# The order of ten score products in a fused attention and feed-forward kernel, and the maxima taken from them

## The chip, the core and the metric

The kernel runs on one core of a Trainium2 chip. A core has a matrix engine (TensorE, PE in the profile, with its weight loads as a row of their own, PEld), a vector engine (VectorE, DVE), an activation engine (ScalarE, ACT), a general engine (GpSimd, POOL), and a queue that issues DMAs (SyncE, SP). Each engine runs its own instructions in the order of the program and waits for others by semaphores. TensorE writes its results to PSUM, eight banks of 512 floats on each of 128 partitions; VectorE and ScalarE read them there. The metric is the device time of one execution in microseconds (us), the median of several runs.

## What is computed

Block-causal attention over 8 batches with 8 heads each, 576 positions of 64 numbers, and behind it a feed-forward layer of width 2048 with a SiLU between its two products:

```python
scores = 0.125 * q @ k^T                     # 576 x 576 for each head
mask: block_i >= block_j, blocks of 64
attn = exp(scores - max) / (sum + 1e-09)
x = (attn @ v), heads side by side           # 4608 x 512
h = x @ w_in;  out = (h / (1 + exp(-h))) @ w_out
```

## The kernel before

A float32 product is made of reduced-precision ones: a number is split into a high part and the rest, and high by high, high by rest and rest by high are added up in PSUM. The attention of the first two blocks of 64 queries is done early and apart. The other 448 queries of each head are the work of a **unit**, u0 to u63, one for each head of each batch. In the stretch from about 80 to 553 us the units run one behind another, mixed with the first feed-forward product of the batches that are done (token `ffn`, line 1071). Behind it comes the second feed-forward product (line 1148).

The order of all of this on every engine is written out by hand: ORDER is a list of tokens such as `u48.scores`, which are run in turn, and each engine gets its instructions in that order. No scheduler moves anything. Around the hand-over from unit 47 to unit 48 it reads:

```python
u47.gather u46.sums:1 keep u47.top ffn u45.inverse u47.spread u48.split_q save u47.wide ffn keep u50.load u47.sub:0 u47.sub:1
u47.exp:0 u48.scores save u47.sub:2 u47.exp:1 u48.max:0 u47.exp:2 u47.pv u48.max:1 u49.split_hi u47.add:0 u48.max:2 u47.add:1
```

What a unit does, step by step:

- `split_hi`, `split_k`, `split_q` (lines 690 to 703): ScalarE and GpSimd make the high parts and the rests of q and k.
- `scores` (line 705): ten products on TensorE, the score of keys by queries, turned so that 128 keys lie on the partitions. There are five groups of keys. Each sees only the queries that its mask allows, so its products are 448, 448, 320, 192 or 64 wide; each group has two products (with q's high part, and with its rest), each with a weight load ahead of it. SEG says for each piece which group of keys it is, its first column, its first query and its width; PASSES says the order of the ten products.
- Three PSUM banks take them (BANKS): the first holds the piece of 448 queries of key group 0, the second the pieces of 320 and 192, the third the other piece of 448 and the one of 64. Four banks go round: with `(3 * u.i + k) % NS`, a unit's second bank is the first bank of the unit before, and its third bank is the second bank of the unit before.
- `max:0`, `max:1`, `max:2` (line 719, the instruction is in the helper at line 656): VectorE takes maxima over the keys of each 32 from the banks into Mx; `half_max` (line 748) does the half-masked squares of 64 keys, two at a time; the last reduction makes mj (line 731).
- `gather`, `top`, `spread`, `wide`: the maxima of the four groups of 32 partitions are brought together by copies on ScalarE (mj, m), reduced, spread again and broadcast to MR.
- `sub:0`, `sub:1`, `sub:2` (line 758): VectorE subtracts the maxima from the scores of the first, second and third bank; this is the last reading of a bank. `sub:1` and `sub:2` end with a `half_sub` (line 752, instruction at 754). The order of sub:1 and sub:2 differs from unit to unit.
- `exp`, `add`, `sums`: ScalarE takes the exponentials (line 771), GpSimd and VectorE their sums. `pv` (line 816) multiplies them with v, `mult` divides by the sums, `x_hi` and `x_lo` make the rows of x.

Semaphores guard a bank as a whole: a reader waits for the last product that is written to the bank, the next writer for its last reader.

```python
SEG = [(0, 0, 0, 448), (2, 448, 128, 320), (3, 768, 256, 192), (1, 960, 0, 448), (4, 1408, 384, 64)]
PASSES = [(i, k, (0, 128)) for i in range(5) for k in range(2)]
BANKS = [(0, 448), (448, 960), (960, 1472)]
```

Of the kernel before, what the change touches and what calls it, by code (L numbers as in the profile page):

```python
# [14 lines left out]
ALU = mybir.AluOpType  # L15
# [41 lines left out]
SEG = [(0, 0, 0, 448), (2, 448, 128, 320), (3, 768, 256, 192), (1, 960, 0, 448), (4, 1408, 384, 64)]  # L57
COLS = 1472

if ROWS:  # L60
    LOWS = [(64, 0, 256), (0, 256, 576)]
    FULL, LOW, HIGH = (0, 128), (0, 64), (64, 128)
    PASSES = [(0, 0, FULL), (1, 0, FULL), (2, 0, FULL), (0, 1, LOW), (1, 1, HIGH), (2, 1, HIGH), (3, 0, FULL), (3, 1, FULL), (4, 0, FULL), (4, 1, FULL)]
else:
    LOWS = [(64, 0, 576)]
    PASSES = [(i, k, (0, 128)) for i in range(5) for k in range(2)]
PV = [0, 3, 1, 2, 4]
BANKS = [(0, 448), (448, 960), (960, 1472)]

# [368 lines left out]
def blocks32(ap):  # L438
    return ap.rearrange("p (b r) -> p b r", r=32)
# [9 lines left out]
def attn_ffn(ctx: ExitStack, tc: tile.TileContext, qk, v, qk0, v0, qk1, v1, w_in, w_out, out):  # L449
# [46 lines left out]
    Mx = sp.tile([P, NQB, 5], F32, tag="Mx", name="Mx")  # L496
# [157 lines left out]
    def ttr(out, in_, op):  # L654

        nc.vector.tensor_reduce(out=out, in_=in_, axis=AX.X, op=op, apply_transpose=True)  # L656
# [12 lines left out]
    class Unit:  # L669
# [35 lines left out]
        def scores(u):  # L705
            banks = [bank((0, 1, 2, 3, "C")[(3 * u.i + k) % NS]) for k in range(3)]

            def ps(c, w, r=P):
                i = max(i for i in range(3) if BANKS[i][0] <= c)
                return banks[i][:r, c - BANKS[i][0] : c - BANKS[i][0] + w]  # L710

            u.ps = ps
            for seg, qq, r in PASSES:
                j, c, q0, w = SEG[seg]
                m = min(P, S - j * P)
                q, r = (u.qh, u.ql)[qq], slice(*r)
                nc.tensor.matmul(u.ps(c, w, m), u.kk[r, j * P : j * P + m], q[r, q0 : q0 + w], start=qq == 0 and not (ROWS and seg == 2), stop=qq == 1 and not (ROWS and seg == 1), skip_group_check=ROWS)  # L717

        def max(u, k):
            if k == 0:  # L720
                ttr(Mx[:, :, 0], blocks32(u.ps(0, NQ)), ALU.max)
            elif k == 1:
                for j, c, q0, w in SEG[1:3]:
                    ttr(Mx[:, q0 // 32 + 2 :, j], blocks32(u.ps(c + 64, w - 64)), ALU.max)
                u.half_max(0)
            else:
                j, c, q0, w = SEG[3]
                ttr(Mx[:, q0 // 32 + 2 :, j], blocks32(u.ps(c + 64, w - 64)), ALU.max)
                u.half_max(1)
                u.mj = sp.tile([P, 4, NQB], F32, tag="mj", name="mj")  # L730
                nc.vector.tensor_reduce(out=u.mj[:, 0], in_=Mx, axis=AX.X, op=ALU.max)
# [510 lines left out]
    for token in ORDER.split():  # L1242
# [3 lines left out]
        elif method:  # L1246
            method, _, k = method.partition(":")
# [47 lines left out]
```

## Time and profile before

| | |
|---|---|
| median of 3 runs | 989.66 us (989.62 to 989.88) |
| span of the profiled execution | 987.9 us |
| TensorE: products, weight loads | 978.8 us, 887.4 us busy |
| VectorE, ScalarE, GpSimd | 790.0, 688.6, 596.7 us busy |
| the 640 score products (line 717) | first at 80.6, last at 545.4 us |
| maxima (line 656, Mx) | 384 instructions, 130.0 us |

The profile shows one execution, from its first instruction to its last; the 1.8 us between its span and the median of the runs lie around it. A row of a timeline has the start, the time taken, the engine, the line, the operation, what is written and read, its shape and count; idle time of the engine ahead of it stands in brackets with what ended it. Rows of equal instructions that follow each other are merged. Products overlap and their ends are modelled, so the start of one and the start of the next say more than the time taken.

### The profile page before, as it was taken

How to read it: one execution, taken by the hardware profiler on the slowest of the kernel's cores; microseconds unless marked ns; L12 is line 12 of the kernel's file. 1: busy time of each engine (PE TensorE's matmuls, PEld its weight loads, DVE VectorE, ACT ScalarE, POOL GpSimd, SP SyncE). 2: the span in 40 equal slices, each digit the busy share in tenths (PEclk: the TensorE clock that was granted, in tenths of full speed). 3: DMA queues.
4: the chain of work that ended last, by engine and by line, in shares of the span. 5: the costliest groups of instructions: out<-in, count | busy, mean ns of one | idle time of the engine just before them, and what ended most of it. 6: DMA issues, size and time to landing. Idle time of an engine off the chain costs nothing.

```text
span 987.9 us, 20770 instructions
## 1 busy us (share of the span) xinstructions
PE 978.8 (99%) x6938; PEld 887.4 (90%) x6938; DVE 790.0 (80%) x2001; ACT 688.6 (70%) x1525; POOL 596.7 (60%) x706
## 2 busy tenths in 40 slices
PE   8999999999999999999999999999999999999998
PEld 7788778888888888888988899999999999999998
DVE  6977998999989899989999766788667767776651
ACT  4867767777777777777777556987666666666650
POOL 5558886877878878877787444554433434344430
PEclk9999999999999999999999999999999999999999
DMA  9965455556555556555554467555445444454411
GB/s 356 373 188 177 142 160 143 157 141 169 152 146 162 148 152 160 145 157 155 143 165 126 141 205 219 193 158 157 130 114 150 129 129 129 126 151 123 127 54 44
DMA packets 109803, 155.51 MB, mean 157 GB/s; under 512 B 18560, under 2 KB 83072, under 8 KB 109696
## 3 DMA queue, kind: packets, MB, share of 16 engines
q1 hardware_dynamic: 109696, 154.18, 52.7%
q8 instruction: 55, 0.90, 0.4%
q14 instruction: 52, 0.43, 0.1%
HBM read 106.95 MB, written 47.19 MB: 156 GB/s over the span
## 4 chain that ended last, share of the span: by engine, by line
PE 95%; DMA 3%; DVE 1%; SPq 0%; issue 0%; ACT 0%; DVEq 0%
PE h L1071 40%; PE S L1148 26%; PE c L1148 10%; PE S L717 9%; PE U L822 5%; PE SC L822 4%; DMA qk<-in_qk_dram 1%; DMA wst<-in_moe_w_in_dram 1%; DMA v<-in_v_dram 1%; PE S L1002 0%; PE S L1043 0%; PE S L879 0%; DVE SC L560 0%; DVE SC L556 0%; DVE wm L566 0%; DVE rr L1023 0%
## 5 line engine op out<-in xcount | busy, mean ns | idle before, releaser
L1071 PE MATMUL h<-x,wi 128*128 128x448 f32 (+2 forms) x1968 | 418.9, 369 | 0.0
L1071 PEld LDWEIGHTS h<-x,wi 128*128 128x128 f32 x1968 | 357.9, 188 | 34.6 <-issue 0.5
L656 DVE TRANSPOSE_TENSOR_REDUCE Mx<-S 64x4 f32<-64x128 f32 (+4 forms) x384 | 130.0, 396 | 7.6 <-PE S L717 6.9
L771 ACT ACTIVATE p<-T 128x512 f32<-128x512 f32 (+1 forms) x192 | 114.7, 613 | 26.7 <-DVE T L760 16.7
L1077 ACT COPY g<-h 128x448 f32<-128x448 f32 (+1 forms) x160 | 86.4, 540 | 38.7 <-PE h L1071 27.5
L777 POOL TENSOR_TENSOR pa<-p 128x448 f32<-128x448 f32 x64 | 73.7, 1151 | 61.1 <-ACT p L771 59.0
L1136 POOL TENSOR_TENSOR x<-raw,x 128x512 fp32r<-128x512 f32 (+1 forms) x58 | 58.8, 1017 | 80.6 <-ACT x L1132 74.9
L1136 POOL TENSOR_TENSOR wi<-raw,wi 128x512 fp32r<-128x512 f32 (+1 forms) x56 | 56.8, 1019 | 75.9 <-ACT wi L1132 71.3
L698 POOL TENSOR_TENSOR qh<-qk,qh 64x576 fp32r<-64x576 f32 x64 | 91.2, 1424 | 9.0 <-POOL pa L780 3.7
L717 PE MATMUL S<-qh 128*128 128x448 f32 (+3 forms) x320 | 92.6, 302 | 0.0
L717 PE MATMUL S<-ql,qh 128*128 128x448 f32 (+3 forms) x320 | 83.7, 306 | 0.0
L692 ACT CAST qh<-qk 128x1024 fp32r<-128x1024 f32 x64 | 67.1, 1049 | 23.1 <-PE S L717 9.5
L1099 ACT ACTIVATE raw<-raw 128x1024 f32<-128x1024 f32 x72 | 76.5, 1063 | 0.0
L702 POOL TENSOR_TENSOR ql<-qk,qh 128x448 fp32r<-128x448 f32 x64 | 73.7, 1151 | 3.8 <-ACT qh L692 1.0
L763 DVE TENSOR_TENSOR T<-S,MR 128x256 f32<-128x256 f32 (+2 forms) x192 | 73.5, 410 | 0.0
L717 PEld LDWEIGHTS S<-ql,qh 128*128 128x128 f32 (+1 forms) x320 | 57.0, 178 | 6.3 <-POOL ql L702 0.2
L717 PEld LDWEIGHTS S<-qh 128*128 128x128 f32 (+1 forms) x320 | 56.9, 178 | 3.3
L780 POOL TENSOR_TENSOR pa<-pa,p 128x320 f32<-128x320 f32 x64 | 55.9, 874 | 4.9 <-ACT p L771 0.2
L1148 PE MATMUL S<-tb,x 128*128 128x256 f32 x450 | 58.8, 283 | 0.0
L1136 POOL TENSOR_TENSOR gc<-raw,gc 128x512 fp32r<-128x512 f32 (+1 forms) x30 | 30.4, 1018 | 43.4 <-ACT gc L1132 39.6
L1148 PEld LDWEIGHTS S<-tb,x 128*128 128x128 f32 x450 | 56.1, 192 | 0.0
L742 ACT COPY m<-m 32x14 f32<-32x14 f32 x192 | 38.8, 202 | 22.0 <-DVE m L738 20.0
(211 smaller groups left out, 2063.6 us busy)
## 6 DMA issues: line engine op xcount, KB each, us to landing
qk<-in_qk_dram SPq DMA_DIRECT2D x128, 256.0 KB, 3.8
gdb<-g SPq DMA_DIRECT2D x128, 224.0 KB, 2.3
raw<-gdb SPq DMA_DIRECT2D x64, 256.0 KB, 3.2
v<-in_v_dram SPq DMA_DIRECT2D x64, 160.0 KB, 2.5
wst<-in_moe_w_in_dram SPq DMA_DIRECT2D x16, 512.0 KB, 8.6
wst<-in_moe_w_out_dram SPq DMA_DIRECT2D x16, 512.0 KB, 4.4
gd<-g SPq DMA_DIRECT2D x32, 256.0 KB, 3.6
raw<-gd SPq DMA_DIRECT2D x32, 256.0 KB, 3.5
```

The source lines that it names most:

```text
L656: nc.vector.tensor_reduce(out=out, in_=in_, axis=AX.X, op=op, apply_transpose=True)
L698: nc.gpsimd.tensor_tensor(out=u.qh[r, c], in0=u.raw[r, c], in1=u.qh[r, c], op=ALU.subtract)
L702: nc.gpsimd.tensor_tensor(out=u.ql, in0=u.raw[:, :NQ], in1=u.qh[:, :NQ], op=ALU.subtract)
L717: nc.tensor.matmul(u.ps(c, w, m), u.kk[r, j * P : j * P + m], q[r, q0 : q0 + w], start=qq == 0 and not (ROWS and seg == 2), stop=qq == 1 a ...
L771: nc.scalar.activation(u.p[:, c:e], u.T[:, c:e], AF.Exp, scale=SCALE)
L777: nc.gpsimd.tensor_tensor(out=u.pa, in0=u.p[:, :NQ], in1=u.p[:, 960 : 960 + NQ], op=ALU.add)
L822: nc.tensor.matmul(U[64 * e : 64 * e + 64, q0 : q0 + w], y.vv[:, e, j], z.p[:, c : c + w], start=n == 0, stop=n == 4)
L1071: nc.tensor.matmul(o, wi[wt][:, c, w], x_of(g, c, xt), start=c + k == 0, stop=c == CT - 1 and k == 2)
L1077: nc.scalar.copy(g, hs.pop(z)[:, :n])
L1099: nc.scalar.activation(u.raw, u.raw, AF.Silu)
L1136: e.tensor_tensor(out=u.goal(1, k), in0=u.source(k), in1=u.goal(0, k), op=ALU.subtract)
L1148: nc.tensor.matmul(o, quarter(u.g[a], j)[:, P * e : P * e + P], quarter(turned[d].g[b], TORDER[FACTOR[pr]]), start=u.q == 0 and i % 2 == 0 ...
```

## The change

The five pieces are computed in the order 0, 3, 1, 2, 4 of SEG, by falling width: 448, 448, 320, 192, 64, two products each. The third bank's wide piece moves ahead of both pieces of the second bank; the 64-wide piece, in the third bank too, stays last. The maxima are regrouped: max:1 now takes the wide piece of the third bank, and max:2 takes the two pieces of the second bank and both half-masked sets. ORDER is the same, and so are the numbers computed.

```diff
 else:
     LOWS = [(64, 0, 576)]
-    PASSES = [(i, k, (0, 128)) for i in range(5) for k in range(2)]
+    PASSES = [(i, k, (0, 128)) for i in (0, 3, 1, 2, 4) for k in range(2)]
...
             if k == 0:
                 ttr(Mx[:, :, 0], blocks32(u.ps(0, NQ)), ALU.max)
             elif k == 1:
+                j, c, q0, w = SEG[3]
+                ttr(Mx[:, q0 // 32 + 2 :, j], blocks32(u.ps(c + 64, w - 64)), ALU.max)
+            else:
                 for j, c, q0, w in SEG[1:3]:
                     ttr(Mx[:, q0 // 32 + 2 :, j], blocks32(u.ps(c + 64, w - 64)), ALU.max)
                 u.half_max(0)
-            else:
-                j, c, q0, w = SEG[3]
-                ttr(Mx[:, q0 // 32 + 2 :, j], blocks32(u.ps(c + 64, w - 64)), ALU.max)
                 u.half_max(1)
```

TensorE at unit 48, before and after with the semaphores waited for. S_6117, S_6118 and S_6119 are the unit's first, second and third bank; the sign - marks rows of before, + rows of the change:

```order
 L717 MATMUL S_6117<-qh 128x448 [waits Pool_49]
 L717 MATMUL S_6117<-ql,qh 128x448 [waits Pool_49]
-L717 MATMUL S_6118<-qh 128x320 [waits DVE_49]
+L717 MATMUL S_6119<-qh 128x448 [waits DVE_49,PE_49]
+L717 MATMUL S_6119<-ql,qh 128x448
+L717 MATMUL S_6118<-qh 128x320
 L717 MATMUL S_6118<-ql,qh 128x320
 L717 MATMUL S_6118<-qh 128x192
 L717 MATMUL S_6118<-ql,qh 128x192
-L717 MATMUL S_6119<-qh 128x448 [waits DVE_49,PE_49]
-L717 MATMUL S_6119<-ql,qh 128x448
 L717 MATMUL S_6119<-qh 64x64
```

The two 448-wide products of the third bank, and the wait for VectorE that they carry, moved from the seventh and eighth place to the third and fourth. The wait that the second bank's first product had of its own is gone, since the third bank's covers it.

VectorE at the same unit, its maxima:

```order
 L656 TENSOR_REDUCE Mx<-S_6117 128x14 [waits PE_49]
-L656 TENSOR_REDUCE Mx<-S_6118 128x8 [waits PE_49]
+L656 TENSOR_REDUCE Mx<-S_6119 128x12 [waits PE_49]
+L656 TENSOR_REDUCE Mx<-S_6118 128x8
 L656 TENSOR_REDUCE Mx<-S_6118 128x4
 L656 TENSOR_REDUCE Mx<-S_6118 64x2x2
-L656 TENSOR_REDUCE Mx<-S_6119 128x12 [waits PE_49]
 L656 TENSOR_REDUCE Mx<-S_6119 64x2x2
 L731 TENSOR_REDUCE mj<-Mx 128x14 [waits DVE_49]
```

The reduction of the third bank moved ahead of the three of the second; it is now the second one of the unit and the last that waits for TensorE. ScalarE, GpSimd and the DMA queue have the same instructions in the same order as before.

## The prediction

> **What bounds the kernel now.** I began with the page's table of busy times and then asked for the same times in three stretches: start, attention (0.08 to 0.553 ms), and the rest.
>
> ```profile
> span 987.9 us, 20770 instructions
> PE 978.8 (99%) x6938; PEld 887.4 (90%) x6938; DVE 790.0 (80%) x2001; ACT 688.6 (70%) x1525; POOL 596.7 (60%) x706
> ```
>
> ```profile
> 80.00:553.00 473.00, 473.00 (x2710) 400.96 (x2709) 431.01 (x1279) 354.17 (x887) 375.88 (x478) 1.00 0.54 151
> 553.00:988.00 435.00, 431.31 (x3377) 424.01 (x3376) 298.69 (x620) 280.74 (x519) 173.71 (x178) 1.00 0.47 139
> ```
>
> TensorE is busy in all of the 473.00 us of the attention stretch and in 431.31 of the 435.00 behind it, at the full clock (1.00). So whatever TensorE loses in a unit is not made good later: it has no idle time to give back. VectorE is the runner-up in the attention stretch: 431.01 of 473.00, some 42 us idle over 64 units. All that follows is one question: does the new order make TensorE wait? Before, it hardly does: the view of the product line names one wait of 0.2 us in 640 products, and the waits run the other way, VectorE for TensorE.
>
> ```profile
>   POOL ql L702: 0.2, 1
> ```
>
> ```profile
> ACT g L1077 <- PE h L1071: 27.5, 46, 1.4
> ...
> DVE MR L660 <- ACT m L742: 15.2, 27, 1.3
> ...
> DVE Mx L656 <- PE S L717: 6.9, 21, 0.8
> ```
>
> **One hand-over, unit 47 to 48.** The timelines of TensorE, then of VectorE:
>
> ```profile
> 427.49 0.36 PE L717 MATMUL S<-qh 128*128 128x448 f32 x1
> ...
> 428.18 0.25 PE L717 MATMUL S<-qh 128*128 128x192 f32 x1
> 428.26 0.28 PE L717 MATMUL S<-ql,qh 128*128 128x192 f32 x1
> 428.38 0.39 PE L717 MATMUL S<-qh 128*128 128x448 f32 x1
> 428.60 0.36 PE L717 MATMUL S<-ql,qh 128*128 128x448 f32 x1
> 428.80 0.19 PE L717 MATMUL S<-qh 128*64 128x64 f32 x1
> 428.83 0.22 PE L717 MATMUL S<-ql,qh 128*64 128x64 f32 x1
> ...
> 433.84 0.37 PE L717 MATMUL S<-qh 128*128 128x448 f32 x1
> ...
> 434.24 0.31 PE L717 MATMUL S<-qh 128*128 128x320 f32 x1
> ...
> 434.74 0.39 PE L717 MATMUL S<-qh 128*128 128x448 f32 x1
> ```
>
> ```profile
> 428.09 2.03 DVE L656 TRANSPOSE_TENSOR_REDUCE Mx<-S 128x14 f32<-128x448 f32 x6
> ...
> 428.66 0.41 DVE L656 TRANSPOSE_TENSOR_REDUCE Mx<-S 128x8 f32<-128x256 f32 x1
> ...
> 433.42 0.61 DVE L763 TENSOR_TENSOR T<-S,MR 128x256 f32<-128x256 f32 x2
> 433.95 0.27 DVE L754 TENSOR_TENSOR T<-S,MR 64x128 f32<-64x128 f32 x1
> ```
>
> Count from a unit's first product. The first maximum starts at 428.09 - 427.49 = 0.60, the second at 428.66, 1.17. The sixth product ends at 428.26 + 0.28, 1.05, so the second maximum did not wait. The tenth ends at 428.83 + 0.22, 1.56. In unit 48 the third product starts 0.40 in (434.24 - 433.84), the seventh 0.90 in.
>
> **Part 1, the second maximum waits for the tenth product.** In the new order the first reduction on the third bank carries a wait and those on the second bank, whose last product is the eighth, carry none: the one wait covers the whole unit, as the 64-wide products end in the third bank. TensorE's end to VectorE's start costs 0.03 to 0.04 us (first maximum 0.60, second product's end about 0.56), so the second maximum starts at 1.60 at the earliest, where it was 1.17: 0.43 us later wherever VectorE is early. Read so for every unit, 31 of the 64 have a delay of 0.35 or more (first unit 0, last unit 60, rows below: 1.17 and 1.18 before), 13 of 0.1 to 0.35, and 20, where VectorE comes late anyway, next to none: 17 us in all. It is idle time of VectorE, so not yet a loss; but queued behind it, in order, stand the other maxima, mj, the broadcast and the three subtractions that free the banks.
>
> ```profile
> 80.58 0.36 PE L717 MATMUL S<-qh 128*128 128x448 f32 x1
> ...
> 81.75 0.41 DVE L656 TRANSPOSE_TENSOR_REDUCE Mx<-S 128x8 f32<-128x256 f32 x1
> ...
> 522.15 0.36 PE L717 MATMUL S<-qh 128*128 128x448 f32 x1
> ...
> 523.33 0.41 DVE L656 TRANSPOSE_TENSOR_REDUCE Mx<-S 128x8 f32<-128x256 f32 x1
> ```
>
> The Trainium skill, PSUM — Partial Sum Buffer, section "PSUM bank collisions raise a hardware error", has it that TensorE writing and VectorE reading one bank on the same partitions collide whatever columns they touch, and asks for semaphores by bank. By that rule the wait for the tenth product cannot be thinned out; with guards by columns, the second maximum would wait for product four and the sum below would be the +2.7 of the rival without delay. The order agrees with the rule; no run here shows a collision.
>
> **Part 2, TensorE needs the bank earlier.** The third bank of a unit is the second one of the unit before, free after the half subtraction that closes sub:1. Before, the seventh product waits for it (0.90 in), now the third (0.40 in): 0.50 less slack. For unit 48 it is free at 433.95 + 0.27 = 434.22, against 434.24. What a release costs is seen at the one hand-over that was late before, unit 10 to 11 (VectorE, weight loads, products):
>
> ```profile
> 164.19 0.27 DVE L754 TENSOR_TENSOR T<-S,MR 64x128 f32<-64x128 f32 x1
> ...
> 164.37 0.19 PEld L717 LDWEIGHTS S<-ql,qh 128*128 128x128 f32 x1
> 164.57 0.19 PEld L717 LDWEIGHTS S<-qh 128*128 128x128 f32 x1
> ...
> 164.46 0.28 PE L717 MATMUL S<-ql,qh 128*128 128x192 f32 x1
> 164.61 0.44 PE L717 MATMUL S<-qh 128*128 128x448 f32 x1
> ```
>
> The subtraction ends at 164.46, the load of the waiting product's weights starts at 164.57, 0.11 later; a load leads its product by 0.09 in the row above (164.37 to 164.46). So release to product is 0.20 us, and a third product stalls by v - 0.20, v being the end of the half subtraction minus the next unit's first product (0.40 in, less 0.20).
>
> The Trainium skill, TensorE: Matmul & The Clock Gate, "Step-by-step: what each phase is for", says that TensorE pulls weight loads ahead of matmuls in flight, which speaks for the change: the weights would lie ready while the product waits. The row disagrees, its load started only after the release; by the rule the price would be the 0.05 of the third rival.
>
> I read v at all 63 hand-overs. Class A, 0.36 to 0.78, has 16 (first unit 1 to 2, last 62 to 63, shown; most have a short unit of 6.35 us); class B, 0.08 to 0.32, has 21 (first unit 0 to 1, shown third); class C, below zero, 26 (48 to 49 shown last).
>
> ```profile
> 94.89 0.27 DVE L754 TENSOR_TENSOR T<-S,MR 64x128 f32<-64x128 f32 x1
> ...
> 94.77 0.36 PE L717 MATMUL S<-qh 128*128 128x448 f32 x1
> ...
> 544.14 0.27 DVE L754 TENSOR_TENSOR T<-S,MR 64x128 f32<-64x128 f32 x1
> ...
> 544.02 0.36 PE L717 MATMUL S<-qh 128*128 128x448 f32 x1
> ...
> 87.66 0.27 DVE L754 TENSOR_TENSOR T<-S,MR 64x128 f32<-64x128 f32 x1
> ...
> 87.80 0.37 PE L717 MATMUL S<-qh 128*128 128x448 f32 x1
> ...
> 440.97 0.27 DVE L754 TENSOR_TENSOR T<-S,MR 64x128 f32<-64x128 f32 x1
> ...
> 441.78 0.36 PE L717 MATMUL S<-qh 128*128 128x448 f32 x1
> ```
>
> - Class A, mean v 0.43. Without any delay of VectorE: 3.7 us in all. With part 1's delay (mean 0.37 there): 16 x (0.43 + 0.37 - 0.20) = 9.6. I take 9.6: in the shown unit VectorE runs through from the maxima to sub:1.
> - Class B, mean v 0.21, mean delay 0.26: 0.6 without delay, 5.6 with all of it. Here I take 3. VectorE waits for ScalarE's copies of m in 27 units (15.2 us), and ScalarE itself is held by the copy of h, which waits for TensorE (27.5 us); such a pause swallows the delay.
> - Class C: 0, at most 0.3.
>
> Sum 12.6 us; ends 4.3 and 15.5.
>
> **Part 3, the narrow products.** Products six to eight start at 428.26, 428.38, 428.60: 0.34 for steps that elsewhere cost 0.08 (192 behind 192) and 0.20 (448 behind 448), so 0.06 is lost behind the two narrow products, 0.051 by the median of all units: a 192-wide product is shorter than the load of the next 128 weight columns. In the new order the second of them is followed by a 64-column load, and only the first still pays: half, 0.025 x 64 = 1.6 us saved. The ends are 0 and 0.051 x 64 = 3.3.
>
> The same instructions run otherwise, on the same engines; SP's queue, POOL and ScalarE keep their order. **Sum: 12.6 - 1.6 = +11.0 us.** The profiled span is 987.9, the median run 989.66; the 1.8 around it is taken as fixed. 989.66 + 11.0 = 1000.7.
>
> **Rivals.**
> - All delay reaches TensorE, and no narrow product gains: +15.5, 1005.2. For it: VectorE's 91% in the stretch. Against: the pauses of class B.
> - No delay reaches it, because the pauses swallow all of part 1: 4.3 - 1.6 = +2.7, 992.4. Against: class A has no such pause.
> - The weights are loaded ahead of the wait, so a release costs 0.05, a little above the 0.03 to 0.04 seen the other way: thresholds rise to 0.35, class A gives 7.2 and B half of 3.0, 8.7 - 1.6 = +7.1, 996.8. Against: the row at 164.57.
> - Both of the last two: 1.3 - 1.6 = -0.3, 989.4, no change.
> - Faster: the narrow products gain all of 3.3 at the unit's end, and stalls stay at 1.3: -2.0, 987.7. It decides where stalls total under 1.3 us, which takes v below 0.35 everywhere but in class A.
> - The change doing something else than it says: the order shows that it does; nothing left for it.
>
> **How the numbers follow.** Forecast 0.52 (996.5 to 1003.5), full delay 0.19, early weights 0.10, no delay 0.09, no change 0.06, faster 0.04. A measurement tells about 0.2%, 2 us. Faster 0.04; same 0.07, with the low edge of "no delay"; slower 0.89. The range 992.5 to 1005.5 leaves out about 0.15 below and 0.05 above.
>
> **What would show it.** In the profile after: VectorE waiting for products at the second maximum in some 40 units, about 17 us where it was 6.9 for all maxima; gaps of up to 0.6 us before third products, 12 us in all, most behind short units, with VectorE's subtraction as releaser; the step into the 64-wide product at 0.09 where the step out of the narrow pair was 0.12. I am wrong if third products start 0.40 in at the short units, or if the loss sits in another line.

## The result, and the profile after

| | before | after |
|---|---|---|
| median | 989.64 us (4 runs) | 1004.0 us (1003.79 to 1004.07, 4 runs) |
| span of the profiled execution | 987.9 us | 1002.1 us |
| first product of unit 0 to first product of unit 63 | 463.4 us | 477.5 us |

The change makes the kernel slower: 1.0145 times the time before, 95% interval 1.0131 to 1.016. The forecast was 1000.7, its range 992.5 to 1005.5. All of the loss, 14.1 us, arises between the first products of unit 0 and unit 63.

The page's span and busy times of after, its chain of work that ended last, and the attention stretch:

```profile
span 1002.1 us, 20770 instructions
...
PE 986.0 (98%) x6938; PEld 886.0 (88%) x6938; DVE 794.4 (79%) x2001; ACT 688.9 (69%) x1525; POOL 596.8 (60%) x706
...
PE 83%; DVE 11%; DMA 2%; ACT 1%; issue 1%; POOL 0%; SPq 0%; ACTq 0%; POOLq 0%; DVEq 0%
```

```profile
80.00:553.00 473.00, 465.78 (x2637) 386.87 (x2636) 422.16 (x1240) 344.18 (x860) 366.94 (x466) 1.00 0.53 149
```

TensorE's busy time in the page tells only half: 986.0 of 1002.1, 7 us more idle than before. A product's modelled row (0.37) is longer than its step to the next one (0.20), so the first 0.17 us of a stall still count as busy. The chain tells more. Before, it was TensorE nearly throughout:

```profile
PE 95%; DMA 3%; DVE 1%; SPq 0%; issue 0%; ACT 0%; DVEq 0%
```

Now 11% of it lies on VectorE. In the 473 us of the window 2637 products were made, where it was 2710. Who waited for whom, after (total, times, longest):

```profile
DVE Mx L656 <- PE S L717: 23.0, 66, 0.8
...
ACT g L1077 <- PE h L1071: 19.6, 36, 1.4
...
PEld S L717 <- PE S L717: 17.1, 30, 0.8
...
DVE MR L660 <- ACT m L742: 15.2, 29, 1.3
...
PE S L717 <- DVE T L754: 6.9, 19, 0.5
```

VectorE waits for score products 23.0 us where it was 6.9, and TensorE, which had one wait of 0.2 us on its score line, waits there too, most of it in two rows: its weight loads (17.1) and its products (6.9), which overlap and must not be added. The row of the loads names a product as releaser because the load waits for two semaphores and that one is matched; the timeline shows who came last. The hand-over from unit 47 to 48, on TensorE's products, its weight loads, and VectorE:

```profile
438.17 0.37 PE L717 MATMUL S<-qh 128*128 128x448 f32 x1
438.37 0.37 PE L717 MATMUL S<-ql,qh 128*128 128x448 f32 x1
438.88 0.44 PE L717 MATMUL S<-qh 128*128 128x448 f32 x1
439.16 0.37 PE L717 MATMUL S<-ql,qh 128*128 128x448 f32 x1
439.36 0.30 PE L717 MATMUL S<-qh 128*128 128x320 f32 x1
...
439.88 0.22 PE L717 MATMUL S<-ql,qh 128*64 128x64 f32 x1
...
444.88 0.37 PE L717 MATMUL S<-qh 128*128 128x448 f32 x1
445.08 0.37 PE L717 MATMUL S<-ql,qh 128*128 128x448 f32 x1
445.90 0.44 PE L717 MATMUL S<-qh 128*128 128x448 f32 x1 [0.45 <-DVE T L754]
446.18 0.37 PE L717 MATMUL S<-ql,qh 128*128 128x448 f32 x1
```

```profile
444.88 0.19 PEld L717 LDWEIGHTS S<-ql,qh 128*128 128x128 f32 x1
445.87 0.19 PEld L717 LDWEIGHTS S<-qh 128*128 128x128 f32 x1 [0.80 <-PE S L717]
```

```profile
438.46 0.27 DVE L754 TENSOR_TENSOR T<-S,MR 64x128 f32<-64x128 f32 x1
438.78 0.65 DVE L656 TRANSPOSE_TENSOR_REDUCE Mx<-S 128x14 f32<-128x448 f32 x1
440.14 1.50 DVE L656 TRANSPOSE_TENSOR_REDUCE Mx<-S 128x12 f32<-128x384 f32 x5 [0.71 <-PE S L717]
...
444.95 0.61 DVE L763 TENSOR_TENSOR T<-S,MR 128x256 f32<-128x256 f32 x2
445.48 0.27 DVE L754 TENSOR_TENSOR T<-S,MR 64x128 f32<-64x128 f32 x1
```

The half subtraction that frees the bank ends at 445.75 (445.48 + 0.27), the weights of unit 48's third product are loaded from 445.87, the product starts at 445.90, 1.02 after the first one, where 0.40 would be free of waits. Behind it the next product comes at 0.28 instead of 0.20, so the stall costs 0.62 + 0.08 = 0.70 us.

Measured so, from a unit's first to its fifth product against what these steps take without a wait, for all 63 hand-overs and by the classes of the prediction:

| | forecast | ends given | measured |
|---|---|---|---|
| class A, 16 hand-overs | 9.6 | 3.7, 9.6 | 9.9 |
| class B, 21 | 3 | 0.6, 5.6 | 5.6 |
| class C, 26 | 0 | 0, 0.3 | 0.9 |
| stalls in all | 12.6 | 4.3, 15.5 | 16.4, at 40 hand-overs over 0.05 |
| narrow products | -1.6 | -3.3, 0 | some -1.7: what is left of the 14.1 (0.6 of the stalls lie behind unit 63's first product) |

### The profile page after: what moved, and what is told of

It reads as the page before. It is cut to its first block, busy times and chain, and to the rows that moved or that the text cites. A ratio compares the mean times of both kernels' runs of the same rounds, so it can differ in the third digit from the quotient of the medians.

```text
span 1002.1 us, 20770 instructions
## 1 busy us (share of the span) xinstructions
PE 986.0 (98%) x6938; PEld 886.0 (88%) x6938; DVE 794.4 (79%) x2001; ACT 688.9 (69%) x1525; POOL 596.8 (60%) x706
## 4 chain that ended last, share of the span: by engine, by line
PE 83%; DVE 11%; DMA 2%; ACT 1%; issue 1%; POOL 0%; SPq 0%; ACTq 0%; POOLq 0%; DVEq 0%
PE h L1071 29%; PE S L1148 26%; PE c L1148 10%; PE S L717 9%; PE U L822 5%; PE SC L822 3%; DVE Mx L656 2%; DVE MR L660 2%; DVE T L763 2%; DMA qk<-in_qk_dram 1%; DVE T L760 1%; DVE Dx L656 1%; DMA wst<-in_moe_w_in_dram 1%; DVE T L754 1%; PE S L1002 1%
## 5 line engine op out<-in xcount | busy, mean ns | idle before, releaser
L656 DVE TRANSPOSE_TENSOR_REDUCE Mx<-S 64x4 f32<-64x128 f32 (+4 forms) x384 | 136.3, 406 | 23.6 <-PE S L717 23.0
L1077 ACT COPY g<-h 128x448 f32<-128x448 f32 (+1 forms) x160 | 86.4, 540 | 30.1 <-PE h L1071 19.6
L717 PEld LDWEIGHTS S<-qh 128*128 128x128 f32 (+1 forms) x320 | 56.8, 178 | 22.8 <-PE S L717 17.1
L665 ACT COPY mj<-mj 32x14 f32<-32x14 f32 x192 | 38.5, 201 | 35.4 <-DVE mj L731 33.2
```

The costliest lines, as they stand in the source:

```text
L1077: nc.scalar.copy(g, hs.pop(z)[:, :n])
```

## The experiments

Seven kernels that compute the same numbers in another order, each with a profile, and a last one that came out of them. Beside each time stands its ratio to the median of before on the same chip, with a 95% interval. That median is 989.84 us for the runs with sub:1 first, with both and with the fifth product, 989.62 for the last run, and 989.51 for the others.

**The maxima as before, in the new product order.** Against the change:

```diff
             elif k == 1:
-                j, c, q0, w = SEG[3]
...
+                for j, c, q0, w in SEG[1:3]:
...
+                u.half_max(0)
```

> The new product order with the maxima grouped as before: the second maximum is on the second bank and waits for the eighth product, which ends some 0.1 us ahead of the tenth. Theory (both together: TensorE's third product needs the bank 0.5 us earlier, and VectorE frees it up to 0.42 us later since its second maximum waits for the tenth product): the delay per unit falls from 0.42 to about 0.31 where VectorE is early, the stalls of third products from 16.4 to about 13 us, the time from 1004.0 to about 1000.5. Rival A (the earlier need of the bank alone makes the loss, VectorE's delay is swallowed): no change, 1004. Rival B (VectorE's delay alone makes the loss, wherever the bank is needed): a quarter less of it, also about 1000.5, so this run does not tell B from the theory; the next one does.

Measured: 1000.89 us, 1.0113 (1.0097 to 1.0128). The stalls, measured as above, are 13.1 us. Less delay of VectorE, less loss, by the amount expected; the rival that the earlier need of the bank does it alone, 1004, falls.

**The maxima alone, in the old product order.** Against the change:

```diff
-    PASSES = [(i, k, (0, 128)) for i in (0, 3, 1, 2, 4) for k in range(2)]
+    PASSES = [(i, k, (0, 128)) for i in range(5) for k in range(2)]
```

> The product order of before with the new grouping of the maxima: the second maximum is on the third bank and waits for the tenth product, but TensorE needs the freed bank only at its seventh product again. Theory: VectorE waits for products about 20 us in all, as with the full change, but the bank comes in time at most hand-overs; stalls of 1 to 3 us, 990.6 to 992.6. Rival A (order alone): 989.6. Rival B (VectorE's delay alone): the whole loss, about 1004.

Measured: 991.86 us, 1.0022 (1.0014 to 1.0031). The second maximum starts 1.79 us after the unit's first product in the mean, where it is 1.38 before and 1.89 with the full change: VectorE is almost as late, and yet only 2.3 us are lost. VectorE's waits in that profile:

```profile
DVE Mx L656 <- PE S L717: 11.4, 36, 0.4
```

TensorE's waits on the score line come to 0.3 us in that view, which leaves out the part of a stall that a product's row covers; by the steps, unit 0 to unit 63 takes 465.9 us, 2.4 more than before, all of it behind the sixth product of the units. (The 20 us expected of VectorE's waits were too many: once it is late, it has less left to wait for.) VectorE's delay alone makes a sixth of the loss.

**The third bank made whole early.** Order 448, 448, 64, 320, 192 with the maxima of the change:

```diff
-    PASSES = [(i, k, (0, 128)) for i in (0, 3, 1, 2, 4) for k in range(2)]
+    PASSES = [(i, k, (0, 128)) for i in (0, 3, 4, 1, 2) for k in range(2)]
```

> Order 0, 3, 4, 1, 2: the two 64-wide products follow their bank's 448-wide ones, so the third bank is whole after the sixth product; the maxima are grouped as in the change. The second maximum then waits for the sixth product, which ends where it did before, so VectorE is not delayed; TensorE still needs the freed bank at its third product. Theory: only hand-overs that were late by themselves stall, 4 to 5 us in all, nothing saved on narrow products: 993 to 995. Rival A (the earlier need alone): about 1004. Rival B (the delay alone): 989 to 990.

Measured: 995.92 us, 1.0063 (1.0049 to 1.0076). The second maximum is back at 1.41 us. Stalls of 5.9 us are left. The time is some 1 us above what was expected: the stalls are 0.9 above the 4 to 5, and the runs on the 64-wide products below show another 0.8 ahead of pv.

**sub:1 ahead of sub:2 everywhere, with the full change.** In 21 units, as here:

```diff
-ffn u46.sub:2 keep u46.exp:0 u46.sub:1 save
+ffn u46.sub:1 keep u46.exp:0 u46.sub:2 save
```

> The full change, and in the 21 units whose subtractions stand in the order 0, 2, 1 the tokens of sub:1 and sub:2 are swapped, so that the bank that the next unit's third product needs is freed some 0.8 us earlier. Theory (the third product waits for the end of sub:1): the stalls behind these units, 5.5 us of the 16.4 in the changed kernel's profile, go, the others stay: 998.5 to 999.5. Rival (the bank is not what the third product waits for, or the wait moves to the exponentials and GpSimd's sums, which now get the third bank later): no change or worse, 1004.

Measured: 999.43 us, 1.0098 (1.0082 to 1.0113). Stalls 11.4 us, 5.0 less. In the waits of ScalarE and TensorE:

```profile
ACT p L771 <- DVE T L754: 14.8, 22, 0.8
...
PEld S L717 <- PE S L717: 10.5, 17, 0.8
...
PE S L717 <- DVE T L754: 4.9, 12, 0.4
```

The third product does wait for the end of sub:1. The rival was right that the exponentials would now wait: ScalarE waits 14.8 us for the half subtraction of sub:2, which is later, where it was 0.3 in the changed kernel. But that is idle time of ScalarE, and it took nothing of the gain away.

**Both: the bank whole early, and sub:1 first.** (The diffs of the two runs above together.)

> The order 0, 3, 4, 1, 2 with the maxima of the change (VectorE not delayed) and sub:1 ahead of sub:2 everywhere. Theory: of the run with that order alone (995.9) the stalls behind the 21 units go, about 2 us; what is left are the short units, 0.2 us each, and what this order costs on products ahead of the pv products: 993.5 to 994.5. Rival (the swap does nothing): 995.9.

Measured: 994.37 us, 1.0046 (1.0032 to 1.0059). As expected.

**The bank needed at the fifth product.** To the run with the maxima as before:

```diff
-    PASSES = [(i, k, (0, 128)) for i in (0, 3, 1, 2, 4) for k in range(2)]
+    PASSES = [(i, k, (0, 128)) for i in (0, 1, 3, 2, 4) for k in range(2)]
```

> Order 0, 1, 3, 2, 4 with the maxima grouped as before: the freed bank is needed at the fifth product (0.69 us in, where it was 0.90 before and is 0.40 in the change), and the second maximum waits for the eighth product, as in the run with the new order and the old grouping (1000.9). Theory: with VectorE's delay the same, 0.29 us more slack takes most stalls away; 3 to 4 us are left and some of the gain on narrow products stays: 991.5 to 993. Rival (VectorE's delay alone makes the loss): 1000.9.

Measured: 993.05 us, 1.0032 (1.002 to 1.0045), at the upper end of what was expected. TensorE's waits on the score line:

```profile
PEld S L717 <- PE S L717: 4.3, 15, 0.3
```

The runs in one table, by when TensorE needs the bank (in a unit in which nothing waits) and when VectorE takes the second maximum (mean of 64 units), both counted from the unit's first product:

| run | bank needed | second maximum | us |
|---|---|---|---|
| before | 0.90 | 1.38 | 989.6 |
| maxima alone | 0.90 | 1.79 | 991.9 |
| fifth product | 0.69 | 1.69 | 993.1 |
| bank whole early | 0.40 | 1.41 | 995.9 |
| maxima as before | 0.40 | 1.77 | 1000.9 |
| the change | 0.40 | 1.89 | 1004.0 |

Where the bank is needed at the same place, a later second maximum takes longer; where the second maximum is about as late (1.69 to 1.79), an earlier need takes longer. The maxima alone cost 2.3 us, the earlier need of the bank alone some 6, both together 14.4, more than the sum of the two.

**The narrow products alone.** The 64-wide products behind the 192-wide ones, all else as before:

```diff
-    PASSES = [(i, k, (0, 128)) for i in range(5) for k in range(2)]
+    PASSES = [(i, k, (0, 128)) for i in (0, 1, 2, 4, 3) for k in range(2)]
```

> Order 0, 1, 2, 4, 3 with the maxima of before: the 64-wide products follow the 192-wide ones, so only one 192-wide product is followed by a 128-column weight load; the third bank is needed at the seventh product as before, and the second maximum waits for the sixth. Theory: no new wait, and the 0.02 us per unit that the change saves on narrow products stays, 1.3 us: 988.3. Rival (that gain belongs to the falling order as a whole, or is given back at the 448-wide products behind the 64-wide ones): 989.6.

Measured: 990.53 us, 1.0005 (0.9996 to 1.0014): no difference, where 988.3 was expected. Unit 44, which pv products follow, in this run and then before:

```profile
404.04 0.36 PE L717 MATMUL S<-qh 128*128 128x448 f32 x1
...
405.32 0.37 PE L717 MATMUL S<-ql,qh 128*128 128x448 f32 x1
405.61 0.97 PE L822 MATMUL U<-p,v 128*64 128x448 f32 x4
```

```profile
404.40 0.37 PE L717 MATMUL S<-qh 128*128 128x448 f32 x1
...
405.76 0.22 PE L717 MATMUL S<-ql,qh 128*64 128x64 f32 x1
405.91 0.60 PE L822 MATMUL U<-p,v 128*64 128x448 f32 x2
```

From the first score product to the first pv product it is 1.57 us here and 1.51 before. The step from a 448-wide product into pv is 0.29, 0.09 more than into another 448-wide one; with the 64-wide products last, the unit is 0.06 shorter. Over the medians of all units: 0.064 us lost in each of the 15 units ahead of pv, 1.0 us, and 0.012 to 0.02 gained in each of the 49 ahead of feed-forward products, 0.6 to 1.0 us, according to which of the products behind the unit is taken. The same loss ahead of pv, 0.056 each, is in the profile of the run with the bank whole early, where 192-wide products are last: 0.8 us.

**The order by what follows.** As that run, but in the 15 units ahead of pv the order of before:

```diff
-            for seg, qq, r in PASSES:
+            for seg, qq, r in (PASSES_PV if u.i in AHEAD_OF_PV else PASSES):
```

> Order 0, 1, 2, 4, 3 in the 49 units that feed-forward products follow, and the order of before in the 15 that pv products follow. In the profile of the run with 0, 1, 2, 4, 3 everywhere a unit with the first product group behind it took 0.012 us less than before, one with pv behind it 0.064 more. Theory (the narrow gain was there, and the step from a 448-wide product into pv took it back): the loss ahead of pv goes, the attention stretch ends about 0.6 us earlier than before, 989.0, which the times can hardly tell from before and the profile's steps can. Rival (no gain on narrow products): as the run with that order everywhere.

Measured: 989.66 us, 1.0002 (0.9993 to 1.0011): no difference. In the profile the loss ahead of pv is gone:

```profile
403.20 0.36 PE L719 MATMUL S<-qh 128*128 128x448 f32 x1
...
404.55 0.22 PE L719 MATMUL S<-ql,qh 128*64 128x64 f32 x1
404.70 0.60 PE L824 MATMUL U<-p,v 128*64 128x448 f32 x2
```

1.50 from the first product to pv, and 462.5 us from unit 0 to unit 63 where before has 463.4 and the run with that order everywhere 463.6. So this small gain, 0.9 us in one profile each, is there in the steps and below what the times can tell. No version measured is faster than the kernel before.

## Why the prediction was right, and where it was short

- **The time** lies in the range, but above the band of the forecast itself (996.5 to 1003.5), and is nearer to the rival with all of the delay (1005.2) than to 1000.7. The stalls, 16.4 us, even lie above their upper end, 15.5; what the narrow products gave back kept the time below that rival. The mechanism was the right one, and too little of the delay was counted.
- **TensorE has nothing to give back.** Right: what was lost among the units, 14.1 us, is what the span grew by, 14.2.
- **The second maximum waits for the tenth product.** Right: VectorE stands idle ahead of it for 17.9 us, in 52 units, where it never did before; 17 us in some 40 units were said. Its mean start moved by more, from 1.38 to 1.89, 33 us over 64 units, since the two parts meet: a unit whose third product stalls has its tenth product later too, and with it its own second maximum. In unit 47 above the third product is 0.31 late, the tenth starts 1.71 in (439.88 - 438.17), and the second maximum begins 1.97 in, not 1.60, after a wait of 0.71. The prediction left this out, but it adds little: the stall moves the next unit's first product back as well.
- **The third product waits for the half subtraction of sub:1.** Right, shown by the rows at 445.48 and 445.90, by the run with sub:1 first (5.0 us of stalls less), and by the fifth product, where nearly the same lateness of VectorE (1.69 against 1.77) costs 3.2 us instead of 11.4.
- **Neither part makes the loss alone.** This follows from the thresholds v - 0.20 and v + delay - 0.20 of the prediction; the table of runs shows it. The rival without delay (+2.7) falls with the run of the maxima as before.
- **The price of a release**, 0.20 us: measured 0.15 to the product (445.75 to 445.90) and 0.08 more at the product behind it, 0.23. The sum of the prediction came near it by two slips: behind a held load the product follows at 0.03 (445.87 to 445.90), not at 0.09, and the 0.08 behind it was not counted. The weights were not loaded ahead of the wait: the load starts 0.12 after the release here, and at none of the 33 hand-overs whose third product is over 0.05 late does it start before the release. The rival of early weights falls. The pull-ahead of weight loads that the Trainium skill describes in TensorE: Matmul & The Clock Gate, "Step-by-step: what each phase is for", is one past matmuls in flight; the traces show none for a load that is itself held by a semaphore.
- **The term that was mis-sized is class B**, 3 us forecast and 5.6 measured, with class C, 0 and 0.9: together 3.5 us, and the forecast was 3.3 short of 1004.0. The step was "such a pause swallows the delay", on which half of class B's delay was left out. On the whole it did not: read at its 21 hand-overs in both profiles, v rose by 0.25 us in the mean, where the delay was 0.26 (in class A 0.37 and 0.37, in class C 0.13 and 0.22). That the mean fits so well is in part luck: in five of the 21 v rose by over 0.1 less than the delay, in five by over 0.1 more, and no run shows why. VectorE's wait for ScalarE's copies of m is 15.2 us in 29 waits after, 15.2 in 27 before. ScalarE waits less for h (19.6 us, it was 27.5), but the pause of VectorE at the broadcast stayed, so it moved along with the maxima that it depends on. That it is the length of the chain from the maxima over the copies to the broadcast, and not ScalarE being held, is the reading that fits; it is not shown, since no run shortened that chain.
- **The narrow products** leave 1.7 us by what remains beside the stalls, close to the 1.6 forecast, but the steps show less: in the 27 units whose third product is not held, the way from the first score product to the products behind the unit is 0.017 us shorter than before by the median, some 1.1 us over all units. The sign that was named for it did not come: the step into the 64-wide product is 0.11, not 0.09. The run of that part alone gave nothing that can be measured, since another end of the unit costs time ahead of pv.

## What to carry to other kernels

A buffer that goes round sets two deadlines, when its next writer needs it and when its last reader lets it go; a reordering that moves both towards each other by less than the slack costs nothing, and by more costs everything on an engine that has no idle time. So before an order is changed within a burst of work, read for each buffer the slack of every hand-over, not the mean: here 16 of 63 hand-overs, 12 of them behind short units, made 9.9 of the 16.4 us. And a semaphore by bank means that the piece written last into a bank sets when any of it can be read: keep the writes to one bank together.

## What the runs showed of the hardware that was not expected

The step from a 448-wide product with 128 weight columns into a pv product with 64 took 0.29 us, into another 448-wide one 0.20; when two 64-wide products lie between, the unit as a whole was 0.06 us shorter. A product that had to wait began 0.15 us after the release, and the one behind it followed at 0.28 instead of 0.20, so that the row of the waiting product alone shows two thirds of the price.
